# New step lengths and new ranks in the plan that orders five engines: attention feeding a two-layer rational network

## The chip, the cores and the metric

The kernel runs on one core of one Trainium2 chip. The metric is the device time of the whole program in microseconds (us), median of the runs shown. In the profile PE is the matrix engine, PEld its weight loads, DVE the vector engine, ACT the engine for activations, POOL a further elementwise engine, and SP the engine that issues all DMAs here.

## The reference, cut to what matters

```python
# q, k, v: batch 8, heads 8, 576 positions, 64 wide
scores = (1 / sqrt(64)) * q @ k.T
mask_plain = (rel >= 0) & (rel < 32)                        # heads 0 to 3
mask_dil = (rel >= 0) & (rel < 128) & (rel % 4 == 0)        # heads 4 to 7
attn = exp(scores - max); attn = attn / (attn.sum(-1) + 1e-9); x = attn @ v
# x as 4608 tokens of 512; w_in 512 x 2048, w_out 2048 x 512
h = x @ w_in
P = a[0] + a[1]*h + a[2]*h**2 + a[3]*h**3
Q = 1.0 + abs(b[0])*abs(h) + abs(b[1])*h**2
g = P / (Q + 1e-6)
return g @ w_out
```

A query sees at most 32 keys, so each head's scores are a narrow band. The weights arrive in double precision.

## The kernel before, in words

**Attention.** Each of the 8 batches is cut into 6 units, numbered 0 to 47. A unit loads its queries and keys (`qk`) and values (`v`), computes banded scores on PE (`s_ps`), a maximum (`mx`) on DVE, the exponential on ACT, a sum and reciprocal (`sm`) on DVE, the division (`p`) on POOL, a transpose, and the product with the values (`o_ps`). The transpose of batches 0 to 2 is done by PE (`t_ps`) and copied out by ACT and DVE (`p_T`, `wo6_T`). From batch 3 on (unit 18) the rows are turned by DVE (`u`), written to memory (`turned`) and read back (`p_T`, `pT`); scores and products then share one tile, `pair`. The result is split into a high part `xh` (ACT) and the rest `xl` (DVE), because PE multiplies a rounded format and full accuracy takes three products. PE runs the product of one unit directly ahead of the scores of the next.

**Weights.** Each of the 16 + 16 pieces of w_in (`wi`) and w_out (`wo`) is turned from double to single precision by one ACT step and three DVE steps (`wi_f`, `wi_b`, `wi_b`, `wi_f`) and split into a high part (ACT or POOL, `wi<-wi_f`) and a rest (POOL).

**Tiles.** The network is 9 chunks of 512 tokens times 16 pieces of the hidden width, 144 tiles. A tile i is: `h` (12 matmuls), then the rational function, which is `a` = |h| and two lines `r`, `t` on ACT, a product `a<-r,a` on POOL, `r` through a logarithm and an exponential on ACT (this divides), five DVE steps of which the last is `a<-a,h`, a high part `gh` on ACT (sometimes POOL), a rest `gl` on POOL, and then `out`, 12 matmuls in four pieces. `h` has two buffers: `h` of tile i+2 can start only after `a<-a,h` of tile i. The order of chunks is: half of chunk 0 (tiles 0 to 7), chunk 1 (8 to 23), the other half of chunk 0 (24 to 31), then chunks 2 to 8. Chunk c needs all six units of batch c.

**What sets the order.** Nothing is ordered at run time: each engine gets a fixed list. `Plan.run` (line 122) builds the lists once, when the program is made. Every step has a length in ns, engines that may do it, and the steps and buffers that it waits for. The plan walks forward in its own time: it takes the engine that could start first, and among the steps that this engine could start within `WINDOW` of that, the one of lowest rank. Ranks of a tile's steps are the tile's number plus an entry of `LATE`. Ranks of attention and weight steps, and of the early tiles' chain, are counted back from the step that needs them (`Plan.due`, line 100), with `DUE` (last unit's due tile and spacing, per batch) and `SLACK` as offsets. Loads of the first phase are issued by SP in the order of their ranks. So the numbers in these tables change no instruction, only its place in its engine's list, and, where a step may run on either of two engines, which one takes it.

## Time and profile before

| What | Value |
|---|---|
| median of 3 runs | 940.06 us (939.92 to 944.67) |
| the profiled execution, its own time | 940.99 us |
| its span, first to last instruction | 939.2 us |
| PE busy | 900.6 us (96%) |
| DVE, ACT, POOL busy | 725.3, 691.6, 478.1 us |
| mean granted PE clock | 0.993 |
| HBM read / written | 67.67 / 16.38 MB |

In a row of the timeline stand the start in us from the span's start, the time until the last instruction of the row ends, engine, line, operation, output <- inputs, partitions and elements, and how many instructions the row merges. In brackets is the idle time of the engine ahead of the row, and what ended it. In a row of windows, each engine's busy time is followed by its number of instructions; the last three columns are the granted PE clock, the share of the DMA engines and GB/s. A wait row is engine, line, what it waited for, total us, times, longest.

### The profile page before, as it was taken

What the parts mean: (1) busy time and instruction counts of PE and PEld (TensorE: products, weight loads), DVE (VectorE), ACT (ScalarE), POOL (GpSimd) and SP (SyncE); (2) the same over time, 40 slices, a digit from 0 to 9 for tenths busy, and PEclk for the clock granted to TensorE, in tenths of its full rate; (3) what the DMA queues carried; (4) which work ended last, traced back from release to release, by engine and by line L of the source; (5) the groups of instructions that cost most, each with busy time, mean ns of one, the idle gap of its engine ahead of it and who ended that gap; (6) DMA issues with size and microseconds to landing.
All of it is one profiled execution on the core that took longest, in us unless ns stands there. A gap on an engine that the chain in (4) does not pass through costs nothing.

```text
span 939.2 us, 19090 instructions
## 1 busy us (share of the span) xinstructions
PE 900.6 (96%) x7277; PEld 726.6 (77%) x7277; DVE 725.3 (77%) x1318; ACT 691.6 (74%) x1245; POOL 478.1 (51%) x409
## 2 busy tenths in 40 slices
PE   5599799999999999999999998999999999999998
PEld 5477577877787778888888887788778887888876
DVE  6988889997777788787787767877787767666665
ACT  4788888877666777777777757776777768777775
POOL 3566567964554445445444444554445435445442
PEclk9989999999999999999999999999999999999999
DMA  9725930025322222322232142222322110001001
GB/s 341 286 71 172 348 142 1 1 88 165 116 101 85 63 91 91 96 74 72 73 116 72 54 143 83 72 71 91 115 91 63 43 46 1 1 1 46 1 0 45
DMA packets 50491, 85.28 MB, mean 91 GB/s; under 512 B 19808, under 2 KB 28384, under 8 KB 50400
## 3 DMA queue, kind: packets, MB, share of 16 engines
q1 hardware_dynamic: 50400, 84.07, 26.7%
q8 instruction: 57, 0.93, 0.4%
q14 instruction: 34, 0.28, 0.1%
HBM read 67.67 MB, written 16.38 MB: 89 GB/s over the span
## 4 chain that ended last, share of the span: by engine, by line
PE 62%; DVE 16%; ACT 10%; POOL 6%; issue 3%; DMA 2%; SPq 0%; POOLq 0%; ACTq 0%; DVEq 0%
PE out L210 28%; PE h L210 27%; ACT r L213 6%; PE pair L210 4%; DVE a L219 4%; POOL a L222 4%; DVE h L219 3%; PE s_ps L210 1%; ACT p L213 1%; ACT a L213 1%; PE o_ps L210 1%; DVE xl L216 1%; DVE mx L337 1%; DVE t L216 1%; DMA p_T<-turned 1%
## 5 line engine op out<-in xcount | busy, mean ns | idle before, releaser
L210 PE MATMUL h<-xh,wi 128*128 128x512 f32 x1136 | 380.8, 397 | 10.2 <-DVE a L219 9.3
L210 PE MATMUL out<-gh,wo 128*128 128x512 f32 x1136 | 355.4, 394 | 0.0
L222 POOL TENSOR_TENSOR a<-r,a 128x512 f32<-128x512 f32 x141 | 182.7, 1296 | 270.0 <-ACT r L213 264.4
L210 PEld LDWEIGHTS h<-xh,wi 128*128 128x128 f32 x1136 | 215.6, 190 | 65.6 <-DVE a L219 19.0
L210 PEld LDWEIGHTS out<-gh,wo 128*128 128x128 f32 x1136 | 209.7, 188 | 44.3
L210 PE MATMUL h<-xl,wi 128*128 128x512 f32 x568 | 223.4, 393 | 0.8 <-DVE xl L216 0.8
L210 PE MATMUL out<-gl,wo 128*128 128x512 f32 x568 | 221.8, 390 | 1.6 <-POOL gl L222 1.6
L222 POOL TENSOR_TENSOR gl<-a,gh 128x512 fp32r<-128x512 f32 x141 | 184.4, 1308 | 34.1 <-ACT gh L213 31.0
L219 DVE SCALAR_TENSOR_TENSOR a<-a,r 128x512 f32<-128x512 f32 x141 | 101.3, 718 | 127.1 <-ACT r L213 127.0
L213 ACT ACTIVATE r<-a,ln_bias 128x512 f32<-128x512 f32 x141 | 102.2, 725 | 80.3 <-POOL a L222 80.3
L213 ACT ACTIVATE a<-h 128x512 f32<-128x512 f32 x140 | 83.5, 596 | 65.7 <-PE h L210 63.7
L213 ACT ACTIVATE r<-a,ab_t 128x512 f32<-128x512 f32 x141 | 114.8, 814 | 19.4 <-DVE h L219 13.2
L210 PEld LDWEIGHTS out<-gl,wo 128*128 128x128 f32 x568 | 106.6, 188 | 25.8 <-POOL gl L222 2.6
L210 PEld LDWEIGHTS h<-xl,wi 128*128 128x128 f32 x568 | 108.1, 190 | 22.6 <-DVE xl L216 1.1
L219 DVE SCALAR_TENSOR_TENSOR h<-h,na_t,r 128x512 f32<-128x512 f32 x142 | 106.7, 752 | 17.0 <-ACT r L213 15.9
L219 DVE SCALAR_TENSOR_TENSOR h<-t,na_t,h 128x512 f32<-128x512 f32 x142 | 107.0, 754 | 4.5
L213 ACT ACTIVATE t<-h,na_t 128x512 f32<-128x512 f32 x142 | 109.8, 773 | 0.5 <-PE h L210 0.4
L213 ACT ACTIVATE r<-r,exp_bias 128x512 f32<-128x512 f32 x144 | 104.0, 722 | 4.1
L216 DVE TENSOR_TENSOR t<-t,h 128x512 f32<-128x512 f32 x142 | 95.8, 675 | 13.9 <-ACT t L213 13.9
L219 DVE SCALAR_TENSOR_TENSOR a<-a,h 128x512 f32<-128x512 f32 x140 | 96.2, 687 | 4.7
L213 ACT ACTIVATE gh<-a 128x512 fp32r<-128x512 f32 x126 | 79.1, 628 | 27.5 <-PE out L210 18.1
L222 POOL TENSOR_TENSOR p<-p,sm 128x384 f32<-128x384 f32 x48 | 44.5, 928 | 87.5 <-DVE sm L371 64.2
(102 smaller groups left out, 706.8 us busy)
## 6 DMA issues: line engine op xcount, KB each, us to landing
v<-in_vp_dram SPq DMA_DIRECT2D x48, 384.0 KB, 3.5
qk<-in_qk_rows_dram SPq DMA_DIRECT2D x30, 448.0 KB, 4.6
out_dram<-os SPq DMA_DIRECT2D x36, 256.0 KB, 2.5
wi_raw<-in_w_in_dram SPq DMA_DIRECT2D x16, 512.0 KB, 9.0
wo_raw<-in_w_out_dram SPq DMA_DIRECT2D x16, 512.0 KB, 9.8
qk<-in_qk_dram SPq DMA_DIRECT2D x12, 608.0 KB, 5.1
turned<-u SPq DMA_DIRECT2D x30, 192.0 KB, 2.0
p_T<-turned SPq DMA_DIRECT2D x30, 96.0 KB, 2.5
```

Of the source, the lines that this page charges most:

```text
L210: pin(nc.tensor.matmul(o, lhs, rhs, start=start, stop=stop))
L213: pin(nc.scalar.activation(o, i, func, **kw))
L216: pin(nc.vector.tensor_tensor(o, x, y, op))
L219: pin(nc.vector.scalar_tensor_tensor(o, x, s, y, op0, op1))
L222: pin(nc.gpsimd.tensor_tensor(o, x, y, op))
L337: pin(nc.vector.tensor_reduce(mx, self.blocks(), axis=AX, op=ALU.max))
```

## The change

The tables `DUE`, `LATE` and `SLACK` get other numbers, and a number of step lengths in the plan are changed (mostly longer; the store of turned rows, `put`, loses an allowance). One rule is added: when PE has to wait in the plan, its step is counted 105 ns longer. No instruction is added or removed by hand; only which of two engines takes a few steps differs.

```diff
-DUE = [(0.94, 0.39), (7.47, 0.67), (31.59, 4.01), (46.12, 2.31), (58.3, 2.05), (80.22, 2.04), (96.72, 1.88), (106.06, 0.47)]
-LATE = {"ab": -8.55, "ql": -4.01, "pl": -1.52, "qq": -2.86, "t1": 1.53, ...
-SLACK = {"sc": -0.39, "qk0": -0.2, "v0": -0.54, "load": -2.56, "wi": 1.44, "wo": 0.87, "w": 0.4, "gl": 0.78, "out": 2.83}
+DUE = [(6.31, 6.42), (18.7, 1.61), (57.71, -13.71), (99.25, 7.55), (59.48, 1.48), (90.0, 3.62), (89.04, -7.31), (128.04, 8.07)]
+LATE = {"ab": 75.94, "ql": -25.43, "pl": 77.35, "qq": -118.12, "t1": 24.94, ...
+SLACK = {"sc": -0.49, "qk0": 5.98, "v0": -15.66, "load": -14.06, "wi": 0.03, "wo": 0.71, "w": -13.91, "gl": 0.86, "out": 2.97}
...
-    PERIOD = 4743.0
+    PERIOD, PE_LATE = 4743.0, 105.0
...
             o.eng = eng
+            if eng == "PE" and start > free.get(eng, 0.0) + 1.0:
+                ns += self.PE_LATE
             free[eng] = start + ns
...
-                ma = mx = op({"DVE": 545}, 0, lambda e: self.max_bank(), sc)
+                ma = mx = op({"DVE": 660}, 0, lambda e: self.max_bank(), sc)
...
-            rc = op({"DVE": 187}, 0, lambda e: self.recip(), sm)
+            rc = op({"DVE": 300}, 0, lambda e: self.recip(), sm)
...
-                pu = op({"SP": 430}, 0, lambda e: self.put(), tr, dma=P * 384 * 4 + 160000)
+                pu = op({"SP": 430}, 0, lambda e: self.put(), tr, dma=P * 384 * 4)
...
-            el = op({"DVE": sum(65 + 2 * c[1] / 0.96 for c, _ in main + left)}, 0, lambda e: self.evac_lo(), eh)
+            el = op({"DVE": sum(120 + 2 * c[1] / 0.96 for c, _ in main + left)}, 0, lambda e: self.evac_lo(), eh)
...
-        lo = op({"POOL": 1253}, 0, lambda e: w_lo(key, e), hi)
+        lo = op({"POOL": 1280}, 0, lambda e: w_lo(key, e), hi)
```

What it does to the lists shows at three places. Lines of the new program are two higher; a number at a name's end only tells buffers apart.

The first is SP's list at the program's start, before the change. The numbers in `q0`, `k0` are units, those in `wi_raw0` pieces of the weights:

```order
L207 DMA mask_t_85<-in_mask_dram 128x384
L207 DMA wi_raw0_106<-in_w_in_dram 128x512
L207 DMA q0_108<-in_qk_dram 128x768
L207 DMA k0_111<-in_qk_dram 128x448
L207 DMA q1_114<-in_qk_dram 128x768
L207 DMA k1_116<-in_qk_dram 128x448
L207 DMA wi_raw1_120<-in_w_in_dram 128x512
```

The same stretch after it:

```order
L209 DMA mask_t_85<-in_mask_dram 128x384
L209 DMA q0_106<-in_qk_dram 128x768
L209 DMA k0_108<-in_qk_dram 128x448
L209 DMA q1_111<-in_qk_dram 128x768
L209 DMA k1_114<-in_qk_dram 128x448
L209 DMA q2_116<-in_qk_dram 128x768
```

The first pieces of the weights have moved behind the queries and keys of all six first units and the values of four. With them the weights' ACT, DVE and POOL steps move back on their lists: POOL does all six divisions `p0` to `p5` before its first step on a weight.

The second is DVE's list at tile 0's chain, before the change:

```order
L216 TENSOR_TENSOR t0_587<-t0_587,h0_525 128x512
L219 SCALAR_TENSOR_TENSOR h0_525<-t0_587,na_t_93,h0_525 128x512
L370 TENSOR_SCALAR sm6_594<-sm6_594 128x3x2
L371 RECIPROCAL sm6_594<-sm6_594 128x6
L219 SCALAR_TENSOR_TENSOR wo_f1_517<-wo_raw1_199,wo_b1_565 128x512
L640 TENSOR_SCALAR wi_b5_610<-wi_f5_523 128x512
L219 SCALAR_TENSOR_TENSOR h0_525<-h0_525,na_t_93,r0_563 128x512
L219 SCALAR_TENSOR_TENSOR wi_b5_610<-wi_raw5_201,wi_b5_610 128x512
L219 SCALAR_TENSOR_TENSOR a0_561<-a0_561,r0_563 128x512
L219 SCALAR_TENSOR_TENSOR a0_561<-a0_561,h0_525 128x512
```

After it:

```order
L218 TENSOR_TENSOR t0_566<-t0_566,h0_510 128x512
L221 SCALAR_TENSOR_TENSOR h0_510<-t0_566,na_t_93,h0_510 128x512
L642 TENSOR_SCALAR wi_b3_578<-wi_f3_477 128x512
L221 SCALAR_TENSOR_TENSOR wi_b3_578<-wi_raw3_190,wi_b3_578 128x512
L221 SCALAR_TENSOR_TENSOR h0_510<-h0_510,na_t_93,r0_561 128x512
L221 SCALAR_TENSOR_TENSOR a0_558<-a0_558,r0_561 128x512
L221 SCALAR_TENSOR_TENSOR a0_558<-a0_558,h0_510 128x512
```

Nothing stands any more between the chain's last three steps, unit 6's reciprocal has moved ahead of the tile, and fewer weights are done by then: 14 of their DVE steps instead of 23. By the last step of tile 5 both lists have done 42.

The third is PE's list around unit 36, before the change, from the unit's scores to its product (`gh79` is the high part of tile 79):

```order
L210 MATMUL pair_2742<-qk36_6193 32x64 x24
L210 MATMUL out4_0_0_5422<-gh79_6303,wo15_2304 128x512 x2
...
L210 MATMUL h80_6402<-xh5_5369,wi0_179 128x512
...
L210 MATMUL h81_6423<-xh5_5369,wi1_362 128x512
...
L210 MATMUL pair_2742<-p_T_88,v36_6364 64x32 x24
L210 MATMUL pair_2742<-qk37_6366 32x64 x24
```

Between them stood `out` of tile 79, `h80` and `h81`, 36 matmuls of 128x512. After the change `h78`, `out` of 75 and 76, `h79`, a quarter of `out` 77 and `h80` stand there, 63 matmuls. The same count from the end of `h8` to the start of `h10` goes from 21 (and one transpose) to 33. In the steady stretches both lists alternate `h` and `out`, and the last 20 rows of every engine's list are the same.

12 lines of the change are left out of this document (6 added, 6 removed).

## The prediction

> **What bounds the kernel now.** First the page's busy times, then a table of windows cut where the program changes stage, then PE's waits.
>
> ```profile
> PE 900.6 (96%) x7277; PEld 726.6 (77%) x7277; DVE 725.3 (77%) x1318; ACT 691.6 (74%) x1245; POOL 478.1 (51%) x409
> ```
> ```profile
> 0.00:33.00 33.00, 19.38 (x315) 17.15 (x316) 23.91 (x57) 18.35 (x71) 12.51 (x23) 1.00 0.95 360
> 33.00:47.30 14.30, 7.46 (x53) 4.90 (x51) 13.64 (x28) 11.29 (x30) 8.38 (x8) 0.94 0.52 198
> 47.30:116.60 69.30, 63.09 (x508) 48.49 (x508) 59.94 (x113) 59.05 (x154) 45.41 (x42) 0.96 0.55 195
> 116.60:200.00 83.40, 82.42 (x392) 66.38 (x393) 79.13 (x117) 68.90 (x109) 64.18 (x51) 0.98 0.15 57
> 200.00:350.00 150.00, 147.19 (x1400) 116.93 (x1399) 115.69 (x226) 106.99 (x209) 74.10 (x68) 1.00 0.33 104
> 560.00:575.00 15.00, 12.05 (x136) 9.57 (x135) 11.41 (x22) 10.77 (x17) 5.45 (x6) 0.89 0.38 119
> 575.00:910.00 335.00, 334.02 (x2390) 271.54 (x2388) 243.32 (x422) 248.62 (x389) 159.74 (x127) 1.00 0.15 48
> ```
> ```profile
> PE h L210 <- DVE a L219: 9.3, 9, 2.8
> PE s_ps L210 <- DMA k<-in_qk_dram: 8.4, 2, 7.2
> PE t_ps L380 <- POOL p L222: 4.9, 5, 3.1
> ```
>
> PE sets the time: it is idle for 939.2 - 900.6 = 38.6 us, and the list change cannot shorten what it does. From 575 to 910 it lacks 1 us of 335. The idle time sits in the start (13.6 of the first 33 us), in 33 to 47.3 (6.8), in 47.3 to 116.6 (6.2), around 565 (3.0) and thinly from 200 to 350 (2.8). The largest wait is `h` for the last DVE step of the tile two before it. From 116.6 to 200 DVE is busy 79.1 of 83.4 us, so PE's full load there hangs on DVE.
>
> **Term 1, the start, to the first matmul of `h2`.** Rows of PE and POOL:
>
> ```profile
> 7.16 4.54 PE L210 MATMUL s_ps<-k,q 128*64 128x64 f32 x48 [7.16 <-DMA k<-in_qk_dram]
> 26.44 1.28 POOL L222 TENSOR_TENSOR wi<-wi_f,wi 128x512 fp32r<-128x512 f32 x1
> 28.15 0.83 POOL L222 TENSOR_TENSOR p<-p,sm 128x384 f32<-128x384 f32 x1 [0.43 <-PE o_ps L210]
> 35.54 0.50 PE L210 MATMUL h<-xl,wi 128*128 128x512 f32 x1 [0.76 <-DVE xl L216]
> 36.82 0.34 PE L210 MATMUL s_ps<-mask_t,ident_b 128*128 128x192 bf16 x2
> 44.04 0.55 PE L380 MATMUL t_ps<-ident,p 128*128 128x128 f32 x3 [3.08 <-POOL p L222]
> 47.25 0.79 PE L210 MATMUL h<-xh,wi 128*128 128x512 f32 x1 [2.67 <-DVE a L219]
> ```
>
> PE's first scores wait for unit 0's keys until 7.16. One piece of weights, 0.52 MB, now follows them instead of preceding them; at the first window's 360 GB/s that is 1.45 us, so PE can start near 5.7. What this is worth shows only at the other end of the stage, where `h0` needs all six units. `h0` ends at 36.82, where unit 6's scores begin. It waited for `xl` of the last first-batch unit, whose chain passes the division at 28.15; that stood on POOL behind weights (26.44) and its reciprocal behind other DVE work. In the new lists the six divisions precede POOL's weights, and unit 6's scores precede `h0`. Fewer weights stand in the way, but `wi0` to `wi2` now do, later. By the order and the rows' lengths I put the end of `h0` at 34.7, a gain of 2.1. The steps of that estimate: the last exponential of the first batch ends near 26.1 in both lists (three of them follow each other on ACT either way); reciprocal 0.35, division 0.83, transpose 0.55, copies 0.5, product 0.92, high part 0.74, rest 0.80, half of `h0` 1.4, hops between engines 0.8, together 6.9; and about 1.7 of weight steps of ACT and DVE that the new lists put between them. Now the same path takes 10.7. Bounds: 0 (the new weights hold it as the old did) and 3.8 (nothing holds it).
>
> From there to `h2` runs tile 0's chain:
>
> ```profile
> 37.48 0.58 ACT L213 ACTIVATE a<-h 128x512 f32<-128x512 f32 x1
> 38.09 0.82 ACT L213 ACTIVATE r<-a,ab_t 128x512 f32<-128x512 f32 x1
> 39.84 1.29 POOL L222 TENSOR_TENSOR a<-r,a 128x512 f32<-128x512 f32 x1
> 42.46 0.74 ACT L213 ACTIVATE r<-a,ln_bias 128x512 f32<-128x512 f32 x1
> 43.23 0.72 ACT L213 ACTIVATE r<-r,exp_bias 128x512 f32<-128x512 f32 x1
> 44.21 0.75 DVE L219 SCALAR_TENSOR_TENSOR h<-h,na_t,r 128x512 f32<-128x512 f32 x1
> 44.87 0.68 DVE L219 SCALAR_TENSOR_TENSOR wi_b<-wi_raw,wi_b 128x512 int32<-128x512 int32 x1
> 45.46 1.01 DVE L219 SCALAR_TENSOR_TENSOR a<-a,r 128x512 f32<-128x512 f32 x1
> 46.51 0.69 DVE L219 SCALAR_TENSOR_TENSOR a<-a,h 128x512 f32<-128x512 f32 x1
> ```
>
> It takes 10.4 us (36.82 to 47.25), of which its own eight steps are 6.6. The rest is queueing: 1.3 us ahead of the logarithm, where ACT does unit 6's exponentials, and 0.6 for a weight step inside the chain. Both are gone from there: the exponentials now precede `a`, which costs about 0.7 at its start, and the DVE steps are adjacent. I take 8.9, a gain of 1.5; bounds 0 and 3. Term 1 is -3.6, bounds 0 and -6.8.
>
> **Term 2, tiles 2 to 10.**
>
> ```profile
> 57.37 0.40 PE L210 MATMUL h<-xh,wi 128*128 128x512 f32 x1
> 60.12 0.62 PE L210 MATMUL out<-gh,wo 128*128 128x512 f32 x2
> 116.55 0.50 PE L210 MATMUL h<-xh,wi 128*128 128x512 f32 x1 [2.81 <-DVE a L219]
> 120.99 0.63 PE L210 MATMUL out<-gh,wo 128*128 128x512 f32 x2
> ```
>
> Twelve matmuls take 2.75 us (57.37 to 60.12), 0.229 each. From the end of `h8` to `h10` the old list had 21 of them and a transpose (0.36), 5.17 us; with the wait of 2.81 the chain needed 7.98. The new list has 33, 7.56 us, so 0.42 is left of the wait: -2.4. `h10` itself took 4.44 us (116.55 to 120.99) with the granted clock down (0.98 over that window): 1.69 over 2.75, which I count as gone with the wait: -1.7.
>
> Against that, 9 weight steps of DVE (0.68 each by the row at 44.87, 6.1 us) and their ACT and POOL steps are moved out of the start into tiles 1 to 5. The stretch from tile 0 to tile 8 then holds 38 of them instead of 32 and three small steps fewer: DVE about 59.9 + 4.1 - 1.2 = 62.8 us, ACT similar. No engine exceeds 63 of the 69.3 us. If the lists keep DVE as busy as now (86%), the stretch grows to 72.6 (+3.3); if the busiest engine is full, it falls to 63 (-6.3). I charge +1.0. Term 2 is -3.1, bounds +3.3 and -6.3.
>
> **Term 3, the boundary at tile 80.**
>
> ```profile
> 565.96 0.27 PE L210 MATMUL pair<-p_T,v 64*64 64x32 f32 x2 [2.54 <-issue]
> 566.63 0.90 PE L210 MATMUL pair<-p_T,v 64*64 64x32 f32 x46 [0.41 <-DMA p_T<-turned]
> 568.24 0.79 PE L210 MATMUL h<-xh,wi 128*128 128x512 f32 x1
> 572.44 0.62 PE L210 MATMUL out<-gh,wo 128*128 128x512 f32 x2
> ```
>
> Unit 36's product waited 2.95 us for its turned rows, and the `h` behind it took 4.20 instead of 2.75 us (568.24 to 572.44; clock 0.89 in the window). Between the unit's scores and product stood 36 matmuls, 8.2 us; 8.2 + 2.95 = 11.2 were needed. Now 63 stand there, 14.4 us. I take -4.4; bounds -4.4 and 0, if the turned rows come 3 us later too.
>
> **Term 4, the rest.** From 200 to 350, 2.8 us of idle time are scattered, and 1 us from 575 to 910. The new list spaces tiles and units more evenly there, but makes `h9` to `h11` tight (30 matmuls, 6.9 us, against the 7.98 that tile 8 needed). I take -0.5, bounds -2.5 and +2.5. From 575 on PE is covered by two buffers of `h` and a distance of 33 to 36 matmuls, and the last rows of all lists agree, so the end costs the same. Where a weight's high part or a chunk's evacuation changes its engine (four rows leave POOL's list, three come to DVE's, one to ACT's) I count nothing: outside tiles 2 to 24 each of these engines has over a fifth of its time free by the windows.
>
> **Sum.** -3.6 - 3.1 - 4.4 - 0.5 = -11.6 against the profiled execution's 940.99 gives 929.4; that execution is 0.9 above the median of the runs, so 928.5. Terms 2 and 4 can lose more easily than gain beyond what I took, so I forecast 929.5.
>
> On the clock: the window rows show it down for waits of 2.8 and 3.0 us. The Trainium skill ("TensorE: Matmul & The Clock Gate", "What's actually happening") has the clock halved after an idle window of about 3.4 us, free-running; by that rule alone the shorter waits would not have cost the 1.69 and 1.45 that I book as recovered, and the sum would be -8.5. This trace shows that they did.
>
> **Rivals.**
>
> *Weights too late (slower).* The new list of SP issues each pair of weights behind a unit's values and next queries, which wait for the unit before to release their buffers. So `wi5` is issued about 1 us after unit 7's scores, and `h5` follows 16.3 us of PE work later.
>
> ```profile
> wi_raw<-in_w_in_dram SPq DMA_DIRECT2D x16, 512.0 KB, 9.0
> qk<-in_qk_dram SPq DMA_DIRECT2D x12, 608.0 KB, 5.1
> ```
>
> At 9.0 us to landing, plus one ACT step, three on DVE and two on POOL (0.7 + 2.1 + 0.6 + 1.3 = 4.7), 14.7 of 16.3 are used. It decides from the point where queueing adds 1.6 us: each of six tiles then waits. At 3 us more than the margin a tile, 18 us on the forecast: 947. For it: DVE and ACT are at 86% there. Against: the 9.0 is a median with many loads queued, while these three in one batch need about 1.6 MB at 0.36 MB/us, 4.5 us, and the clock penalty aside PE has work to take first. Chance 0.13.
>
> *DVE held by POOL.*
>
> ```profile
> 144.58 1.81 DVE L219 SCALAR_TENSOR_TENSOR a<-a,r 128x512 f32<-128x512 f32 x1
> 147.16 0.50 PE L210 MATMUL h<-xh,wi 128*128 128x512 f32 x1 [0.91 <-DVE a L219]
> ```
>
> This step took 1.81 instead of 0.69 us, and `h` waited 0.91 behind it. Moved weight splits on POOL can meet it oftener. At one tile in three of the first 24, 8 x 0.9 = 7 us: 936.5. The few such rows speak against it. Chance 0.08. The Trainium skill ("SBUF — State Buffer", "SBUF: two separate sides") states that a VectorE step with two SBUF inputs and a GpSimd step exclude each other for a whole instruction; the row agrees.
>
> *The moves cancel.* The start gains 1, the dense stretch gives 3 back, only term 3 stays: 938. For it: DVE has 9 us of slack from tile 2 to 10, and takes 3 more. Chance 0.17. That the lists do not change is excluded: all are rearranged.
>
> **How the numbers follow.** Forecast 0.62 (923 to 935), cancelled 0.17 (935 to 942), held DVE 0.08 (933 to 939), late weights 0.13 (942 to 955). What a measurement of this kernel can tell from no change is 0.5%, 4.7 us. Faster by more: 0.62 + 0.05 + 0.03 = 0.70; within: 0.18; slower: 0.12. The range that leaves 2 in 10 out is 922 to 941: all lower bounds together would give 920, late weights lie above.
>
> **What would show it.** Term 1: `h2` starts at 43 to 45 rather than 47.25. Term 2: `h10` starts at 108 to 113 with a wait under 1 us, and the clock column stays at 1.00 after it. Term 3: no wait at unit 36's product, `h80` to `h82` at the plain rate. Late weights would show as waits of `h` or `out` for POOL's `wi` and `wo`, which the old trace does not list. The forecast is wrong if PE's busy time plus its waits does not fall by 7 us, or if new waits of over 2 us appear between tiles 2 and 24.

## The result, and the profile after

The changed kernel takes 938.42 us (median of 10 runs, 935.67 to 939.02). The kernel before, run beside it, takes 943.27 (939.92 to 946.28). The ratio is 0.9947, 95% interval 0.9930 to 0.9963: 0.5% faster, 4.9 us, where 929.5 us and some 11 us were forecast. The profiled execution took 936.79 us, its span 935.0 (939.2 before).

Busy times of the changed kernel, then the table of windows with the cuts that the prediction used (the window 350 to 560, which it left out, included), then PE's waits:

```profile
PE 898.8 (96%) x7277; PEld 725.0 (78%) x7277; DVE 728.9 (78%) x1320; ACT 693.6 (74%) x1247; POOL 473.2 (51%) x405
```
```profile
0.00:33.00 33.00, 21.57 (x344) 18.54 (x345) 21.91 (x58) 19.23 (x73) 9.04 (x20) 1.00 0.87 318
33.00:47.30 14.30, 9.19 (x33) 7.00 (x32) 13.59 (x24) 12.10 (x29) 10.15 (x10) 0.80 0.31 112
47.30:116.60 69.30, 62.36 (x510) 47.52 (x509) 61.70 (x116) 60.57 (x158) 45.78 (x43) 0.99 0.71 261
...
350.00:560.00 210.00, 208.41 (x2058) 167.98 (x2057) 167.66 (x316) 152.31 (x247) 98.14 (x81) 1.00 0.27 87
560.00:575.00 15.00, 15.00 (x156) 12.27 (x155) 13.39 (x24) 11.25 (x18) 8.01 (x7) 1.00 0.40 130
```
```profile
PE s_ps L212 <- DMA k<-in_qk_dram: 6.3, 2, 5.7
PE t_ps L382 <- POOL p L224: 6.3, 8, 2.4
PE h L212 <- DVE a L221: 6.2, 10, 2.7
PE o_ps L212 <- ACT p_T L215: 4.6, 6, 1.1
PE out L212 <- ACT os L215: 2.3, 2, 1.7
```

The window 350 to 560 of the kernel before, for comparison:

```profile
350.00:560.00 210.00, 209.96 (x1987) 171.50 (x1986) 163.66 (x318) 150.44 (x246) 99.67 (x81) 1.00 0.27 85
```

The start and the boundary near 565 became shorter: PE is busy 21.57 of the first 33 us instead of 19.38, and without a gap from 560 to 575. PE's waits of `h` for DVE fell from 9.3 to 6.2 us. But two lines are new in this list: `o_ps` for the copies of `p_T`, and `out` for the copy `os`. And from 350 to 560 PE is now 1.59 us short of full, which the old trace was not (0.04).

The four places of the prediction's terms, in the timeline of PE:

```profile
43.07 0.79 PE L212 MATMUL h<-xh,wi 128*128 128x512 f32 x1 [2.73 <-DVE a L221]
...
112.45 0.50 PE L212 MATMUL h<-xh,wi 128*128 128x512 f32 x1 [0.20 <-DVE a L221]
...
117.90 0.73 PE L212 MATMUL out<-gh,wo 128*128 128x512 f32 x2 [1.72 <-ACT os L215]
...
553.97 0.90 PE L212 MATMUL pair<-p_T,v 64*64 64x32 f32 x48
```

`h2` starts at 43.07 (47.25 before), `h10` at 112.45 with a wait of 0.20 (116.55, 2.81), and unit 36's product runs without a wait.

**An account in equal work.** Clock times of two lists cannot be compared directly, since attention stands elsewhere in them. So I give each matmul a fixed length (0.2272 us for a 512-column one, and so on for the small ones), add these up in the order of issue, 875 us in every kernel, and note when each kernel reaches the same sum. The cuts are at 20 us of such work (just behind the start of `h2`; 47.8 us in the trace before), 77 (just behind that of `h10`, 117.0), 150 (193.6), 300 (350.6), 510 (561.4), 520 (576.2) and the end. A column is named by the end of its stretch in the old trace. A row is the kernel's time minus that of the kernel before, stretch by stretch, in us, and in sum:

```
kernel        to h2  h2-h10  -194   -351   -561   -576    end     sum
the change     -4.2   +0.5   -0.6   +1.2   +4.0   -4.8   -0.3    -4.2
a_lengths      -2.4   +1.4   +0.8   -2.6  +12.5   -4.8   -1.4    +3.4
b_ranks        -2.4   +3.9   +6.0   -0.6   +0.8   -4.8   -1.8    +1.1
c_start        -3.8   +0.2   -0.8   -0.6  +10.1   -4.4   -0.3    +0.4
d_steady       -3.9   +0.3   +0.8   -2.4  +10.3   -4.3   +1.3    +2.2
dose_act       -1.4   +6.7   +5.0   +1.3   +3.7   -4.8   -0.1   +10.4
dose_dve       -1.5   +8.4   +8.8   +1.6   +4.1   -4.8   -0.8   +15.8
dose_pool      -3.0   +3.9  +12.4   +0.9   +3.8   -4.8   -0.5   +12.7
no_low         -4.4   -1.9   +4.3   +1.4   +3.8   -4.8   -0.8    -2.4
no_scale       -4.3   -3.1   -0.8   +1.0   +3.7   -4.8   -0.6    -9.0
hi_act         -3.5   +1.2   +2.2   +1.3   +3.5   -4.8   -0.2    -0.2
pt_dve         -2.9   +3.0   -0.5   +0.7   +4.0   -4.8   -0.5    -1.1
h_dve          -2.6   -0.9   +6.3   +2.0   +4.3   -4.7   +0.2    +4.6
i_pe           -2.8   +0.5   +2.9   -1.8   +4.2   -4.7   -1.4    -2.9
f_g01          -2.5   +1.3   -0.5   -0.1   +4.0   -4.0   +8.2    +6.3
g_oldlate      -3.2   +0.7   -0.5   -0.7   +2.0   -4.1   -0.4    -6.3
l_actold       -2.9   +1.1   +1.8   -0.0   +1.6   -4.7   -1.5    -4.7
j_g01old       -4.6   +1.0   -0.5   +0.1   +2.9   -4.1   -1.9    -7.0
```

Each row is one execution. The change and f_g01, g_oldlate, l_actold, j_g01old have the very same lists until some 280 us, so their first three columns show the scatter of one program: -2.5 to -4.6 in the first, 0.5 to 1.3 in the second, -0.6 to +1.8 in the third. A difference of 1 to 2 us in one of these columns is therefore nothing. The column -561 scatters less: the eight kernels that keep the change's order there (the change, the three dose kernels, no_low, no_scale, hi_act, pt_dve) give +3.5 to +4.1. But in g_oldlate and j_g01old a wait lies beside the cut at 510, and some 0.8 us of theirs may stand in that column or in the next. Against the terms of the prediction, for the change: the start -4.2 (forecast -3.6), tiles 2 to 10 with what follows -0.1 (-3.1), the boundary -4.8 (-4.4), the rest +4.9 (-0.5: it is +1.2, +4.0 and -0.3).

### The profile page after: what moved, and what is told of

It is laid out like the page before. It is cut to its first block, busy times and chain, and to the rows that moved or that the text cites. A ratio compares the mean times of both kernels' runs of the same rounds, so it can differ in the third digit from the quotient of the medians.

```text
span 935.0 us, 19110 instructions
## 1 busy us (share of the span) xinstructions
PE 898.8 (96%) x7277; PEld 725.0 (78%) x7277; DVE 728.9 (78%) x1320; ACT 693.6 (74%) x1247; POOL 473.2 (51%) x405
## 4 chain that ended last, share of the span: by engine, by line
PE 40%; DVE 27%; ACT 15%; POOL 7%; issue 5%; DMA 4%; SPq 1%; POOLq 0%; ACTq 0%; DVEq 0%
PE h L212 19%; PE out L212 18%; ACT r L215 10%; DVE a L221 7%; DVE h L221 6%; POOL a L224 5%; DMA wi_raw<-in_w_in_dram 2%; PE pair L212 2%; DVE t L218 2%; DVE mx L339 2%; DVE xl L218 2%; DVE pair L218 1%; DVE p L218 1%; DVE sm L369 1%; ACT p L215 1%
## 5 line engine op out<-in xcount | busy, mean ns | idle before, releaser
L215 ACT ACTIVATE gh<-a 128x512 fp32r<-128x512 f32 x134 | 84.1, 627 | 14.7 <-PE out L212 11.6
L224 POOL TENSOR_TENSOR p<-p,sm 128x384 f32<-128x384 f32 x48 | 41.9, 873 | 96.2 <-DVE sm L373 63.5
```

The costliest lines, as they stand in the source:

```text
L215: pin(nc.scalar.activation(o, i, func, **kw))
L224: pin(nc.gpsimd.tensor_tensor(o, x, y, op))
```

## The experiments

### Half the change each: ranks, lengths

One kernel has the new ranks and the old lengths, the other the reverse. By a distance the expectations mean the matmul work that PE has between the `h` of a tile and the `h` two tiles later, which waits for the chain of the first.

```diff
 b_ranks: the change, but
-    PERIOD, PE_LATE = 4743.0, 105.0
+    PERIOD = 4743.0
...
-                ma = mx = op({"DVE": 660}, 0, lambda e: self.max_bank(), sc)
+                ma = mx = op({"DVE": 545}, 0, lambda e: self.max_bank(), sc)
... (every other length as before)
 a_lengths: the change, but DUE, LATE and SLACK as before
```

> The change's ranks (DUE, LATE, SLACK) with the old step lengths: one half of the change. Theory (what counts is how many matmuls stand between a tile's scores and the tile two later, wherever the order came from): in the order of this kernel the work ahead of h2 is as in the changed kernel, the product h80 to h82 has no short distance, and only tiles 38, 39 and 112 to 117 have 6.9 to 7.5 us of matmuls where a tile's chain takes 7.7 to 8.4. So nearly the whole change is kept: h2 at 43 to 44 us, no wait at unit 36's product, profiled execution 936 to 939, ratio to the kernel before 0.993 to 0.997. Rival (the lengths bring the gain, the ranks only fit them): the ratio is 0.999 or above, with waits back at tile 80.

> The change's step lengths with the old ranks: the other half. Theory (distances): the distance of 4.40 us of matmuls that the kernel before has behind h80 is found behind h48 here, so its price moves there and is not saved: a wait of 2 to 3 us near 48's product with a stretch at half clock behind it, 4 to 5 us in all. The start has 22.2 us of matmuls ahead of h2 rather than 20.3, with the distance from h0 to h2 grown from 4.21 to 5.03 us, so some 1 us of the start's wait goes. Sum: 0 to -2 us against the kernel before, ratio 0.998 to 1.000. Rival (the lengths bring the gain): ratio 0.995 or below and no wait of over 1 us between tiles 10 and 130.

Measured: b_ranks 942.59 us, ratio 0.9995 (0.9978 to 1.0013); a_lengths 943.52, 1.0010 (0.9998 to 1.0021). Neither half shows a gain; both together give 0.5%. The theory failed for b_ranks. It has no stall at tile 80, as expected (-4.8 in that column), and the best steady part of all. But it loses 3.9 us up to `h10` and 6.0 behind it. Its distances there are within 0.7 us of the change's, except behind `h6` (1.4 us more) and `h8` (1.4 us less). PE's waits are of other things: up to `h10` 8.2 us of unit products for ScalarE, behind it eight waits of `h` for VectorE, 4.6 us in all. So a distance counted on PE alone does not tell whether a tile waits. For a_lengths the theory held: its list has the short distance, 4.40 us of matmuls, behind `h48` instead of `h80`, and it pays there.

### New start with old steady part, and the reverse

```diff
 c_start: the change, but LATE and DUE[3:] as before
 d_steady: the change, but SLACK and DUE[0:3] as before
```

> The changed kernel with the old ranks for the steady part (LATE, and DUE from unit 3 on). Up to h10 its order is that of the changed kernel. Two theories on the 4 us that the changed kernel lost between 350 and 560 us against the kernel before: (1) the new LATE puts attention steps ahead of the tile chain's last steps on VectorE, so many small waits; then they are gone here. (2) They come from something that stays (ScalarE's load, the lengths). Both expect a stall at tile 48, where the order has a distance of 4.40 us: about +4.8 us. So (1): the loss from 350 to 560 us outside that stall is as in the kernel before and the profiled execution 936.8 + 4.8 - 4.0 = 937.6; (2) 941 to 942.

> The changed kernel with the old ranks for the start (DUE of units 0 to 2 and SLACK): new steady part, old start. Theory (the new start wins 4.2 us up to h2 and then loses about 4.5 us in tiles 3 to 7 to the weights' steps and unit 1's and 2's attention, which the new ranks put there): h2 later than 43.1 us by the 1.9 us of matmuls that stand ahead of it here and by 1 to 3 us of wait, h0's distance being 5.03 us; tiles 3 to 7 at 8 us each rather than 9. Up to h10 the sum is within 1.5 us of the changed kernel's 112.5. The distance of 4.40 us stands behind h48: +4.8 us there. Together 939 to 943 for the profiled execution. Rival (the crowding of tiles 3 to 7 is there in any order, since ScalarE has the same work to do): tiles 3 to 7 take 9 us each here too, h10 at 114 to 117, and 943 to 946.

Measured: c_start 939.93, ratio 0.9975 (0.9964 to 0.9986); d_steady 944.72, 1.0020 (1.0008 to 1.0033). Both have the short distance behind `h48`, and the timeline of c_start shows the price there, followed by the row of windows for the time after it:

```profile
366.17 0.27 PE L212 MATMUL pair<-p_T,v 64*64 64x32 f32 x2 [2.88 <-DVE a L221]
366.86 1.50 PE L212 MATMUL pair<-p_T,v 64*64 64x32 f32 x46 [0.42 <-DMA p_T<-turned]
```
```profile
366.30:373.20 6.90, 6.48 (x106) 5.27 (x106) 5.38 (x12) 3.68 (x6) 2.51 (x2) 0.51 0.41 127
```

The waits are 3.3 us, and then the granted clock is at 0.51 for 6.9 us. Between 346 and 405 us c_start loses 6.3 us, a_lengths 6.4, d_steady 6.2 (4.8 were expected, the price at tile 80 in the kernel before). Four lists have one distance of 4.40 us, and four have a stall at that place.

What PE waits for is the unit's turned rows, as the prediction had it, and not the chain of a tile. In the same four lists, and in none of the others, a unit's product stands only 36 matmuls (8.2 us) behind its scores. PE goes on 0.09 us after the first load of the turned rows has landed (at 565.87 us before the change, 366.08 in c_start, 368.35 in a_lengths, 365.98 in d_steady), 10.9 to 11.5 us after the scores. The `DVE a` in the row of c_start had ended 0.3 us before. In f_g01 a unit at 464 us has 48 matmuls (10.9 us) there, and its product waits 0.95 us. The 4.40 us between `h80` and `h82` contain this product, so the two short distances come together in all four lists, and what the shorter distance between tiles would cost alone is not shown there.

Of c_start's two theories on the steady part, the second came true: outside the stall it loses 3.8 us up to 561 (10.1 less 6.3), as much as the change, although its ranks there are the old ones. Its profiled execution took 941.4 us.

On the old start each side was right in part. As the theory had it, d_steady reaches `h2` late, at 46.2 us, and `h10` at 112.6. As the rival had it, tiles 3 to 7 take 9.1 us each (9.5 in the change), not 8. d_steady has 32 of DVE's weight steps between `h2` and `h10` like the kernel before, the change has 38, and both need the same time for the stretch (+0.3 and +0.5). So the number of moved weight steps alone does not set it.

### Which engine holds the stretch from h2 to h10

The wait of `h10` is gone, and yet it is 69.4 us from the start of `h2` to that of `h10` instead of 69.3. PE's waits in it, of the kernel before and of the change:

```profile
PE h L210 <- DVE a L219: 3.8, 2, 2.8
PE out L210 <- POOL gl L222: 1.6, 2, 1.3
PE t_ps L380 <- POOL p L222: 0.7, 1, 0.7
```
```profile
PE o_ps L212 <- ACT p_T L215: 3.7, 4, 1.1
PE out L212 <- POOL wo L224: 1.4, 1, 1.4
PE out L212 <- POOL gl L224: 0.9, 1, 0.9
PE t_ps L382 <- POOL p L224: 0.4, 1, 0.4
PE h L212 <- DVE a L221: 0.2, 1, 0.2
```

6.1 us of waits became 6.6: those of `h` for DVE were replaced by those of unit products for ScalarE's copies and of `out` for a weight. To learn which engine's work is behind this, I did one step of each weight piece twice on one engine, in unchanged lists. (The expectations count 16 pieces; there are 16 + 16, so the second stretch, up to 189 us, gets about as many as the first.)

```diff
 dose_act, in w_scale:
+        act(w, w_words(key)[:, :, 1].bitcast(F32), AF.Abs, scale=2.0**-112)
         act(w, w_words(key)[:, :, 1].bitcast(F32), AF.Abs, scale=2.0**-112)
 dose_dve: the step of w_sign twice; dose_pool: the step of w_lo twice, for wi alone
```

> The changed kernel, in its own order, with one ScalarE step done twice: the first step of each of the 16 weight pieces (wi_f, wo_f; 0.67 us each, 12 of them between 47 and 117 us), so 8.0 us more for ScalarE in that stretch and 2.7 us before it. Theory (ScalarE sets the pace of tiles 3 to 8, since the starts of its step a<-h there stand 9.1 us apart where PE has 7.8 us of matmuls): h10 starts 6 to 8 us later than in the changed kernel, the profiled execution is 943 to 946. Rival 1 (VectorE or the weights' landing sets it): 0 to 2.5 us later. Rival 2 (POOL): the same 0 to 2.5.

> The changed kernel, in its own order, with one VectorE step done twice: the last step of each of the 16 weight pieces (0.63 us each, about 12 of them between 47 and 117 us), so 7.6 us more for VectorE there. VectorE is busy for 61.70 of those 69.3 us, ScalarE for 60.57. Theory (ScalarE sets the pace): h10 0 to 2.5 us later than in the changed kernel, the profiled execution 937 to 940. Rival 1 (VectorE sets the pace, or both in turn): h10 5 to 8 us later, 942 to 945.

> The changed kernel, in its own order, with one POOL step done twice: the last step of the 8 pieces of wi (1.28 us each, 7 of them between 47 and 117 us), so 9.0 us more for POOL there, which is busy for 45.78 of 69.3 us. Theory (ScalarE sets the pace): h10 0 to 2.5 us later, the profiled execution 937 to 940. Rival 2 (POOL's last step of a weight or of the tile chain is what the matmuls wait for): h10 6 to 9 us later, 943 to 946.

Measured: 948.24 us, ratio 1.0056 (1.0041 to 1.0072); 956.60, 1.0142 (1.0128 to 1.0156); 953.59, 1.0113 (1.0099 to 1.0127). The rows of windows, cut just behind the start of `h2`, just behind that of `h10`, and at 150 us of matmul work: the change, dose_act, dose_dve, dose_pool.

```profile
44.20:113.90 69.70, 63.18 (x509) 48.41 (x508) 62.10 (x117) 60.12 (x158) 46.18 (x43) 0.97 0.67 243
113.90:189.30 75.40, 73.14 (x321) 59.47 (x321) 72.83 (x112) 62.20 (x97) 63.71 (x55) 1.00 0.10 39
```
```profile
47.00:122.90 75.90, 65.89 (x509) 49.85 (x508) 62.11 (x117) 69.32 (x172) 45.90 (x43) 0.94 0.64 233
122.90:203.90 81.00, 75.53 (x322) 60.58 (x321) 74.20 (x112) 69.72 (x109) 63.10 (x55) 0.98 0.07 28
```
```profile
46.90:124.50 77.60, 65.72 (x509) 50.76 (x508) 70.97 (x130) 61.26 (x158) 46.26 (x43) 0.93 0.62 225
124.50:209.30 84.80, 77.49 (x322) 59.97 (x321) 81.87 (x126) 62.60 (x97) 63.09 (x55) 0.98 0.07 28
```
```profile
45.30:118.50 73.20, 63.08 (x509) 48.22 (x508) 67.03 (x117) 60.85 (x158) 55.89 (x49) 0.98 0.65 241
118.50:206.90 88.40, 77.71 (x322) 59.73 (x321) 77.27 (x112) 62.76 (x97) 71.34 (x62) 0.98 0.07 25
```

For the first stretch: 9.2 us more on ScalarE cost 6.2 (0.67 for each), 8.9 on VectorE cost 7.9 (0.89), 9.7 on POOL cost 3.5 (0.36). For the second: 0.75, 1.04 and 1.7. All three theories "this engine alone" fail, since the prices of the three add up to 1.9 and 3.5. All three kernels took longer than any range expected of them, with twice as many steps doubled as were counted. A price above 1 for POOL is more than its own time; the group rows below show a reason.

Part of these prices is the clock. Up to `h10` the granted clock is at a half for 8.5 us in dose_act, 10.5 in dose_dve and 3.2 in dose_pool, against 4.1 in the change; behind it, for 3.4 us in each of the three and never in the change. At half clock PE can lose half of the time at most, so by this estimate up to 2.2 of the 6.2 us of dose_act, 3.2 of the 7.9 of dose_dve, and 1.7 of what each of the three costs in the second stretch.

Adding cannot tell a bound from a chain that runs through all engines; taking away can. These two were run for that:

```diff
 no_low leaves out the last bits of each weight, in w_low:
-        stt(bits, w_words(key)[:, :, 0], 29, bits, ALU.logical_shift_right, ALU.bitwise_or)
 no_scale, w_scale only takes its buffer, w_shift reads the raw words:
-        act(w, w_words(key)[:, :, 1].bitcast(F32), AF.Abs, scale=2.0**-112)
```

> The changed kernel in its own order of every queue, without one VectorE step of each weight piece: the last three bits of each weight are not put in, so the output is slightly off. There are 32 pieces, not the 16 I counted before; 0.69 us a step, 5 of them up to h2, 13 from h2 to h10, 14 from there to 189 us. Theory (VectorE's work sets the pace while weights are decoded, as the doubled step cost 0.89 us for each us from h2 to h10 and 1.04 behind): h2 to h10 falls by 6 to 8 us from 69.7; the stretch from 114 to 189 us by 2 to 3, since TensorE has 72.4 us of matmuls in its 75.4; the start by 0 to 2. Profiled execution 924 to 928. Rival (the lists hand the wait on from engine to engine, so that taking work from one gains much less than giving it costs): 2 to 5 us in all, 932 to 935.

> The changed kernel in its own order of every queue, without ScalarE's step of each weight piece (VectorE's first step reads the raw words instead, so the weights' values are wrong and only the time is read): 32 steps of 0.67 us less for ScalarE, 13 of them between h2 and h10. Theory (VectorE sets the pace): h2 to h10 falls by at most 2 us, the whole by 0 to 4: 933 to 937. Rival 1 (ScalarE sets it there, as the doubled step's 0.67 us for each us says): h2 to h10 falls by 5 to 6 us, the whole by 6 to 9: 928 to 931.

Measured: no_low 939.47, ratio 0.9979 (0.9966 to 0.9992), no gain on the change; no_scale 933.22, 0.9916 (0.9887 to 0.9944). The rows of the two stretches, of no_low and of no_scale:

```profile
44.00:111.20 67.20, 62.48 (x509) 47.71 (x508) 55.98 (x105) 59.73 (x158) 46.45 (x43) 0.98 0.68 249
111.20:191.50 80.30, 75.44 (x322) 59.00 (x321) 71.97 (x98) 62.97 (x97) 60.99 (x55) 1.00 0.10 39
```
```profile
44.10:110.10 66.00, 61.55 (x509) 48.01 (x508) 61.78 (x117) 53.48 (x144) 46.11 (x43) 0.98 0.67 244
110.10:185.30 75.20, 73.12 (x322) 59.56 (x321) 73.11 (x113) 56.03 (x85) 63.82 (x55) 1.00 0.13 51
```

In the first stretch VectorE has 12 instructions less in no_low, which takes 6.1 us from its busy time and 2.5 us from the stretch; ScalarE has 14 less in no_scale, 6.6 us of busy time and 3.7 us of the stretch. That is 0.41 and 0.56 for each us, where adding cost 0.89 and 0.67. By the estimate above, up to 0.8 and 1.0 us of these gains is a shorter slow clock (2.5 and 2.2 us at a half instead of 4.1). The stretch scatters by 0.8 us between executions of one program, so for VectorE the two prices differ, and for ScalarE they cannot be told apart. In the second stretch PE is busy for 73.1 of 75.4 us in the change, so no list can win more than 2.3 us: 6.2 us less of ScalarE's busy time win 0.2, while adding cost 0.75 for each us. And fourteen VectorE steps less (9.7 us) make it 4.9 us *longer*.

VectorE does 98 instead of 112 instructions there in no_low and is busy nearly as long as before (71.97, 72.83). The groups of one step, `a<-a,r`, in that stretch (count | total us, mean ns | idle time before): the change, the kernel before, dose_pool, no_low, and what VectorE waits for in no_low:

```profile
L221 DVE SCALAR_TENSOR_TENSOR a<-a,r 128x512 f32<-128x512 f32 x13 | 9.2, 706 | 0.0
```
```profile
L219 DVE SCALAR_TENSOR_TENSOR a<-a,r 128x512 f32<-128x512 f32 x13 | 12.1, 932 | 0.0
```
```profile
L221 DVE SCALAR_TENSOR_TENSOR a<-a,r 128x512 f32<-128x512 f32 x13 | 13.4, 1027 | 0.0
```
```profile
L221 DVE SCALAR_TENSOR_TENSOR a<-a,r 128x512 f32<-128x512 f32 x13 | 17.1, 1314 | 0.0
...
DVE h L221 <- ACT r L215: 6.5, 12, 1.4
```

This is the only VectorE step of the chain whose mean changes, and it is the one that the prediction's second rival named (held while POOL works). One of them in the timeline of no_low, with POOL's step beside it:

```profile
156.17 1.29 POOL L224 TENSOR_TENSOR wo<-wo_f,wo 128x512 fp32r<-128x512 f32 x1
156.47 1.54 DVE L221 SCALAR_TENSOR_TENSOR a<-a,r 128x512 f32<-128x512 f32 x1
```

VectorE comes to it 0.3 us after POOL has begun, and ends 0.55 us after POOL is done. On average each of 13 is held by 0.6 us; the tile chain is that much longer, and VectorE then waits 6.5 us for ScalarE. So the time taken from VectorE comes back as holding and waiting. From `h2` to 189 us, no engine's sum of work is the bound by itself: the tile chain goes through ScalarE, POOL and VectorE in turn, and the lists decide how the turns meet. The rival of no_low, that the lists hand the wait on, fits this best, but not its gain of 2 to 5 us in all: by the ratios no_low is 3.0 us slower than the change. Of no_scale's two expectations for the first stretch, at most 2 us and 5 to 6, neither came true.

Two runs tried to use this: the 20 high parts of weights that POOL does, given to ScalarE, and the second half of the `p_T` copies given to VectorE, each at its old place in the plan.

```diff
 hi_act:
-        hi = op({"ACT": 525, "POOL": 590}, 0, lambda e: w_hi(key, e), steps[-1])
+        hi = op({"ACT": 525, "POOL": 590}, 0, lambda e: w_hi(key, "ACT"), steps[-1])
 pt_dve:
-                p1 = op(place1, 0, lambda e: self.place(1, e), tr, zeroed[alt], Unit.av_of.get(alt))
+                p1 = op(place1, 0, lambda e: self.place(1, "DVE" if b == 1 else e), tr, zeroed[alt], Unit.av_of.get(alt))
```

> The changed kernel in its own order of every queue, except that the 20 high parts of weights which POOL does (0.62 us each; 6 of them between 44 and 114 us, 12 between 114 and 189) are done by ScalarE at the same place of the plan. From the three runs with a step doubled: one us more of ScalarE's time cost 0.67 us in the first stretch and 0.75 in the second; of POOL's 0.36 and 1.7; VectorE's unchanged steps grew by 0.5 us for each us added to POOL. Theory (in the second stretch VectorE is 97% busy and POOL's steps lengthen VectorE's): VectorE's busy time from 114 to 189 us falls by 3 to 4 us and the stretch by 1 to 4; the first stretch grows by 0 to 1.5; profiled execution 933 to 937. Rival (ScalarE's price decides, and POOL's is paid only for the step that ends a weight): 20 x 0.62 x 0.7 = 8.7 us longer, less 2 to 4 for POOL: 941 to 944.

> The changed kernel in its own order of every queue, except that VectorE instead of ScalarE copies the second half of the turned probabilities (p_T, 0.48 us) of units 6 to 11, at the same place of the plan. Between 44 and 114 us TensorE waits 3.7 us for these copies, which ScalarE does one behind the other. Theory (no engine alone holds this stretch, a wait is only handed on): h10 starts within 1.5 us of the changed kernel's 112.5, since VectorE's chain steps come 0.5 us later in their turn; profiled execution 935 to 938. Rival (ScalarE's copies are what this stretch waits for): h10 2 to 3 us earlier, 933 to 935.

Measured: hi_act 940.56, ratio 0.9979 (0.9969 to 0.9989); pt_dve 938.86, 0.9957 (0.9940 to 0.9975). Both are misses. In hi_act the second stretch is 2.7 us longer than in the change, not shorter, and VectorE's busy time did not fall. Up to 1.7 us of that is the clock, at a half for 3.4 us behind a wait of 1.96. ScalarE's price agrees with the direction, though the whole came to 3.0 us by the ratios (4.0 by the profiled executions) rather than the 8.7 less 2 to 4 of the rival. In pt_dve four of the waits for the copies grew to 1.2 to 1.7 us each and `h10` starts at 116.2, 3.8 us late, of which 1.3 are there at `h2` already. Neither theory had that. VectorE's longer queue would agree with its higher price in this stretch, but two of the four waits ended with a step of ScalarE, so the cause is not shown.

### What the steady part lost

In the stretch up to 561 us the change loses 4.0 us. PE's list of waits from 350 to 560 us, empty before the change, has one line:

```profile
PE h L212 <- DVE a L221: 1.3, 3, 0.5
```

One of the three in the timeline, with VectorE around it:

```profile
422.22 0.69 DVE L221 SCALAR_TENSOR_TENSOR a<-a,r 128x512 f32<-128x512 f32 x1 [0.86 <-ACT r L215]
422.84 0.77 DVE L218 TENSOR_TENSOR pair<-pair,mask_t 128x192 f32<-128x192 f32 x2
423.64 0.56 DVE L339 TENSOR_REDUCE mx<-pair 128x6 f32<-128x384 f32 x1
...
426.44 0.72 DVE L221 SCALAR_TENSOR_TENSOR h<-h,na_t,r 128x512 f32<-128x512 f32 x1
427.20 0.69 DVE L221 SCALAR_TENSOR_TENSOR a<-a,h 128x512 f32<-128x512 f32 x1
...
427.94 0.50 PE L212 MATMUL h<-xh,wi 128*128 128x512 f32 x1 [0.55 <-DVE a L221]
```

Two steps of the chain have the same input, `r`. `a<-a,r` (rank of the tile - 3.61) runs at once; `h<-h,na_t,r` (rank + 12.84) stands behind eight rows of attention, 3.6 us, and PE waits for what follows. PE's idle time in the window, 1.6 us, is less than half of the loss. The rest lies in matmuls that the profile shows as busy and that follow each other more slowly; how much of it has the same cause is not shown. Six kernels ask which numbers do this: the old attention lengths of VectorE (h_dve), those of PE (i_pe), the two steps (`g0` and `g1` in LATE) ahead of all attention (f_g01), all of the old LATE (g_oldlate), the old LATE of ScalarE's steps (l_actold), and of the two steps (j_g01old).

```diff
 h_dve: 660 to 545, 300 to 187, sum(120 + ...) to sum(65 + ...)
 i_pe: 370 to 250, 1690 and 1800 to 1350 and 1750, 1000 to 720
 f_g01: LATE "g0": -155.0, "g1": -155.5
 g_oldlate: LATE as before
 l_actold: LATE of "ab", "ql", "pl", "ln", "ex", "gh" as before
 j_g01old: LATE "g0": 2.39, "g1": 0.11 as before
```

> The changed kernel with the three VectorE lengths of the attention put back to the old ones (the row maximum 660 to 545, the reciprocal 300 to 187, the low part's 120 to 65 for a piece). Theory (the longer VectorE lengths give the attention steps earlier ranks, so that on VectorE they stand ahead of the tile chain's step h<-h,na_t,r, which then starts over 2 us after its input in 9 of tiles 48 to 79 where the kernel before has 1): at most 4 such tiles here, and the 3.6 us that the changed kernel lost between 401 and 561 us against the kernel before are down to under 1.5. In its order no distance behind tile 12 is under 7.1 us, so no boundary stall. Profiled execution 932 to 936. Rival (the lengths of the matmul steps or the wait put on PE are the cause): 9 such tiles as before, the same 3 to 4 us lost, 936 to 939.

> The changed kernel with the lengths of the attention's matmul steps put back (scores with product 1690 and 1800 to 1350 and 1750, products and scores alone 1000 to 720, 370 to 250 for a mask on TensorE); the wait length put on PE stays. Theory (the longer matmul lengths make the planner place the attention's VectorE steps ahead of the tile chain's, so the 3 to 6 us lost between 350 and 560 us in every kernel with the new lengths come from them): under 1.5 us lost there, at most 4 of tiles 48 to 79 with h<-h,na_t,r over 2 us behind its input. No distance under 6.8 us behind tile 8. Profiled execution 932 to 935. Rival (the other lengths: the unit's store of turned rows, the wait put on PE): 3 to 4 us lost as before, 936 to 939.

> The changed kernel with the ranks of the tile chain's two VectorE steps h<-h,na_t,r and a<-a,r moved ahead of the attention's (LATE of g0 12.84 to -155.0, of g1 -3.61 to -155.5). Theory (attention steps that stand ahead of these two cause the small waits of h from 350 to 560 us): in tiles 48 to 79 at most 2 start h<-h,na_t,r over 2 us after its input rather than 9, and under 1 us of the 3.6 us is lost from 401 to 561 us, except what a distance of 5.77 us behind h64 costs (8.4 needed, 2 to 3 us). This order also has a distance of 2.74 us behind h112: some 5 us of wait and 2 to 3 of half clock near 790 us. Profiled execution 940 to 944. Rival (the planner's list only moves the attention's delay to the units' products): waits of pair for p_T in place of those of h, nothing gained from 401 to 561 us, 943 to 948.

> The changed kernel with LATE alone put back to the old ranks of the tile chain's steps. Its order up to tile 17 is that of the changed kernel, and no distance behind tile 12 is under 6.85 us, so no stall at tile 48 or 80 (the run with old LATE and old due times had one at 48, 6.3 us between 346 and 401 us). Theory (the loss of small waits from 350 to 560 us comes from LATE and the due times together, both read wrongly): under 1.5 us of it is left, profiled execution 932 to 935. Rival (it comes from the lengths, which stay): 3 to 4 us of it are left, 936 to 939.

> The changed kernel with the old ranks of the tile chain's ScalarE steps alone (ab, ql, pl, ln, ex, gh of LATE); its VectorE steps keep the new ones. All of LATE put back won 2.3 of the 3.6 us lost from 401 to 561 us and 2 us of span. No distance behind tile 12 is under 6.8 us. Theory (ScalarE's ranks cost it: in the new ones a and t of a tile come behind the attention's exponentials and high parts): the gain is here, profiled execution 932 to 935, ratio to the kernel before 0.990 to 0.994. Rival (VectorE's ranks cost it, g0's 12.84 above all): nothing changes, 936 to 938.

> The changed kernel with the old ranks of the two VectorE steps h<-h,na_t,r and a<-a,r alone (g0 12.84 to 2.39, g1 -3.61 to 0.11). No distance behind tile 12 is under 6.8 us. Theory (VectorE's ranks cost the 3.6 us lost from 401 to 561 us): at most 1.5 of it left, profiled execution 932 to 935, ratio 0.990 to 0.994. Rival (ScalarE's ranks cost it): 936 to 938.

Measured, in this order: 945.13 us, ratio 1.0028 (1.0018 to 1.0039); 937.41, 0.9948 (0.9935 to 0.9960); 945.60, 1.0040 (1.0025 to 1.0055); 935.34, 0.9922 (0.9908 to 0.9936); 932.78, 0.9905 (0.9879 to 0.9930); 933.95, 0.9918 (0.9894 to 0.9943).

- The lengths of VectorE's or of PE's attention steps alone are not it: +4.3 and +4.2 in that column, as in the change (+4.0), and 7 and 10 late tiles where at most 4 were expected. h_dve also loses 6.3 us from `h10` to 194, like b_ranks: with the new ranks, that stretch is worse with the old VectorE lengths.
- f_g01 supports the mechanism, in the part of the stretch that its own short distance leaves alone. Only 1 of tiles 48 to 79 has `h<-h,na_t,r` over 2 us behind its input (9 in the change, 1 before). From 350 to 450 us, where its list has no distance under 8.1 us (tiles 49 to 63), PE is full; the change is not, as the second fence shows. In equal work, by the times of the old trace, it loses nothing from 350 to 460 us, where the change loses 2.3. Its price comes elsewhere: 3.1 us from 460 to 480, at a distance of 5.77 us behind `h64` (2 to 3 were expected), and then at one of 2.74 behind `h112`, where the wait is 4.01. So its column is +4.0 too, and its profiled execution, 947.3 us, lies in the range of its rival:

```profile
350.00:450.00 100.00, 100.00 (x883) 81.74 (x883) 79.76 (x152) 73.68 (x120) 47.96 (x40) 1.00 0.26 86
...
768.92 0.50 PE L212 MATMUL h<-xh,wi 128*128 128x512 f32 x1 [4.01 <-DVE a L221]
```
```profile
350.00:450.00 100.00, 99.17 (x962) 79.59 (x961) 80.50 (x153) 73.04 (x119) 46.99 (x39) 1.00 0.27 87
```

- The ranks set its size, in part: g_oldlate loses 2.0, l_actold 1.6, j_g01old 2.9 us in the column. Over this column and the next, which does not depend on the cut, they gain 1.3, 2.3 and 0.4 us on the change. By the ratios, the three beat the change by 2.4 to 4.0 us; l_actold's interval ends where that of the change begins, the other two overlap it a little, and among each other they cannot be told apart. By the ratio both theories of the last pair came true. But the profiled execution of l_actold, 936.3 us and the slowest of its six, lies in its rival's range, and j_g01old has 2.9 us of the loss left where at most 1.5 were expected: its gain comes mostly in other columns. So ScalarE's ranks cost something in this stretch; for VectorE's two it is not shown.
- The new lengths are in every kernel that loses much. With the old lengths the new ranks lose 0.8 (b_ranks). With the new ones, the old LATE and the new DUE lose 2.0 (g_oldlate), the old LATE with the old DUE from batch 3 on 3.8 outside the stall (c_start), and all old ranks 6.1 (a_lengths: 12.5 less 6.4). So the new ranks are not needed for the loss. Which length it is stays open: the 105 ns on a waiting PE and the allowance of the store were never put back alone. Open, too, is how the lateness of the step counts: g_oldlate and l_actold have 11 and 12 tiles with it over 2 us late and lose less than the change with 9. That it matters only where PE has little work in between would fit, but no run tests it.

l_actold, at 932.8 us and 0.9905, has the lowest median of all that ran, both given kernels included.

## Why the prediction was right and wrong

Of the 11.6 us forecast against the profiled execution, 4.2 came. Two terms of the sum failed, term 2 by 3.0 us and term 4 by 5.4; the other two gained 1.0 more than forecast.

**What bounds the kernel: right.** PE sets the time. Its idle time fell by 2.4 us, and its busy time by 1.8 (900.6 to 898.8), with the clock at a half for 6.8 us instead of 13.7.

**Term 1, the start: right, -4.2 for -3.6.** The first scores start at 5.71 (near 5.7 forecast), `h1` follows `h0` at 34.53 (34.7), and the chain to `h2` takes 8.5 us (8.9). Over the five executions of the same list the gain is 3.5 us on average.

**Term 2, tiles 2 to 10: the term that was mis-sized, -0.1 for -3.1.** Its parts on `h10` are right: the wait fell from 2.81 to 0.20 (0.42 forecast), and no half clock followed. The step that failed is "I charge +1.0", in which only the nine weight steps were to cost something, as a share of busy engines. The real cost up to `h10` is about 3 us, the 2.6 us of wait that went and the 0.5 of growth; behind `h10` two new waits of `out` for `os` (2.3 us) took most of what the clock gave back there. I had gone by which engine was full. The runs show that none is the bound alone, that a us added to VectorE or ScalarE costs 0.89 or 0.67 and a us removed brings 0.41 or 0.56, and that the stretch takes 68 to 73 us in every list with this same work. A wait removed at one tile came back at the unit products of the tiles before it.

**Term 3, the boundary at tile 80: right, -4.8 for -4.4.** Its mechanism, a product too close behind its unit's scores for the turned rows to be back, is shown by three lists that have the 36 matmuls at tile 48 and stall there. What was not foreseen is that the place hangs on ranks and lengths together: with either half of the change alone the short distance behind `h80` is gone, and with one of them it comes back behind `h48`.

**Term 4, the rest: wrong, +4.9 for -0.5, the larger miss.** "The new list spaces tiles and units more evenly there" was read from distances on PE, which did become more even. The step that failed is to take even distances on PE for covered waits. VectorE's list was not compared where no wait stood in the old trace: from 350 to 560 us PE was full, so I left that window out of the table. A full stretch can only lose, and this one lost 4.0 us, in part because the last chain steps stand behind attention on VectorE (9 late tiles instead of 1); the rest of the cause is open. The bound of +2.5 was too low for the same reason.

**The rivals.** Late weights: no; PE waits for a weight once up to `h10`, 1.4 us. VectorE held by POOL: not in this change, where the step's mean between `h10` and 190 us fell from 0.93 to 0.71 us, but no_low and dose_pool show the mechanism, with 4 to 8 us more of VectorE's time in 13 steps. "The moves cancel" (938) came nearest, with the cancelling in the steady part more than in the start. Of the two signs of being wrong, "new waits of over 2 us between tiles 2 and 24" did not appear, since the longest is 1.7 us; the other did, with the span shorter by 4.2 us where 7 were asked.

## What to carry to other kernels

When a list is changed, cost the full stretches first: they have no wait to lose, and each engine's list there can only make new ones. Where a chain passes through several busy engines, do not price moved work by the fullest engine; double a step on each, and also take one away, since a price may hold in one direction only, and part of it may be the clock. Lengths and ranks of a static plan are one setting: here neither half, tried alone, showed the gain of the whole.

## What the runs showed of the hardware

**The clock can halve after a wait of 1.8 us.** The granted clock goes to a half for 3.4 us or twice that. In one execution these periods start on one raster: in the kernel before at 45.51, 117.19 and 567.75 us, which are 21 and 132 times 3.413 us apart. The wait of `out` for `os` near 118 us is of nearly one length in ten kernels, so it shows the limit at this place. In l_actold it is 1.78 us, and the window behind it has the clock at 0.50; in j_g01old it is 1.77, and the clock stays full:

```profile
119.84 0.73 PE L212 MATMUL out<-gh,wo 128*128 128x512 f32 x2 [1.78 <-ACT os L215]
...
121.10:124.50 3.40, 3.40 (x10) 2.62 (x9) 3.33 (x6) 1.48 (x3) 3.32 (x4) 0.50 0.10 38
```
```profile
118.08 0.73 PE L212 MATMUL out<-gh,wo 128*128 128x512 f32 x2 [1.77 <-ACT os L215]
...
119.60:123.00 3.40, 3.40 (x16) 2.61 (x14) 3.33 (x6) 2.55 (x4) 3.32 (x4) 1.00 0.06 21
```

After 1.72 to 1.77 us it stayed full in eight kernels, after 1.78 and 1.96 (hi_act) it fell. In both kernels shown, the whole wait lies in the 3.4 us ahead of the window quoted, so about half of that time was idle. Elsewhere the limit is less sharp: in i_pe PE is idle for 1.82 of the 3.41 us from 37.23 and the clock stays full, in dose_act for 1.66 from 69.19 and it falls. The Trainium skill ("TensorE: Matmul & The Clock Gate", "What's actually happening") says that the clock falls after an idle window of about 3.4 us in a free-running raster. The starts and the length of the slow periods agree with such a raster. That the whole window must be idle does not: here half of one was enough, and the prediction's term 3 with its 1.45 us of slow clock rested on that rightly.

**One VectorE step is held by POOL as a whole.** `a<-a,r` takes 0.69 us in most tiles and up to 1.8 us, with 0.6 us more on average over 13 tiles in no_low; its neighbours with `h` among their inputs keep 0.69 and 0.75. The Trainium skill ("SBUF — State Buffer", "SBUF: two separate sides") describes an exclusive lock between a VectorE step with two SBUF inputs and a POOL step, whichever comes first. The trace agrees. What it adds here is that less work on VectorE can cost time (no_low's second stretch, 4.9 us longer): the step then arrives while POOL is busy.
